# Attention with two expert layers: 64-query sets merged into one matmul pair, wider streams in the values' and first gate's matmuls, two groups of sums emitted later

## The chip, the core and the metric

The kernel runs on one core of one Trainium2 chip. The metric is device time in microseconds (us) of one execution, and lower is better. The engines are TensorE (PE for its matmuls, PEld for its weight loads), VectorE (DVE), ScalarE (ACT), GpSimd (POOL) and SyncE (SP, which only issues transfers here). TensorE's clock has two levels, 1.2 and 2.4 GHz; the profile gives the granted clock of a stretch as 0.50 or 1.00.

## What is computed

Windowed attention over 2 batches, 8 heads, 576 positions and 64 columns per head; then a first expert layer, which sends each of the 1152 tokens to the one expert that its gate prefers; then a second expert layer, in which every token goes through all 8 experts, weighted by a matrix that eight rounds of row and column scaling (the Sinkhorn steps) produce from the second gate.

```python
scores = where((rel >= 0) & (rel < 128), scale * q @ k.T + slope_h * (-abs(rel)), -1e9)
attn   = exp(scores - max) / (sum(exp) + 1e-9)
x      = (attn @ v)                                   # 1152 tokens x 512
...
e      = argmax(x @ w_gate, axis=1)                   # first gate; a token keeps its place below the capacity
x1[i]  = gate_w[i] * (relu(x[i] @ w1[e]) @ w2[e])     # first expert layer
...
P      = exp(x1 @ u_gate - max)                       # second gate
for _ in range(8):                                    # the Sinkhorn steps
    P /= P.sum(1, keepdims=True) + 1e-9
    P /= P.sum(0, keepdims=True) + 1e-9
    P *= N / E
out    = sum over e of P[:, e] * (relu(x1 @ u1[e]) @ u2[e])
```

## The kernel before

**Attention.** Queries go in blocks of at most 128. A batch has 576 positions, so it has four blocks of 128 and a last one of 64: of the ten blocks `t`, numbers 4 and 9 have 64 queries. A unit `u` is one block with four of the eight heads (two units per block, so units 8, 9, 18 and 19 are the 64-query sets). For each unit the steps are `scores` (PE), `pick`, `limit` (DVE), `powers` (ACT), `turn_p` (PE transposes of the probabilities), `take_p` (they are moved to SBUF as `pT`, by ACT, DVE and POOL), `values` (PE) and `norm` (DVE). The probabilities of one query block against the block before and against its own are two parts, and `values` adds both in PSUM: for a 64-query block the first part has 128 rows and the second has 64.

In `values` the stationary operand is `pT` of one head (128 or 64 columns wide), and the moving operand is 104 columns of the values (`WIDE`), of which 65 are used: 64 of the head and a column of ones that gives the sum of the powers. The last head of a block has only 65 columns left to stream. `norm` divides by that sum. An fp32 matmul shows in the trace as two records of the same shape.

**First gate.** `turn_x`, `take_x` and `logits` give the gate's logits of a block. The 8 columns of the gate's weights are streamed six times side by side (48 columns), of which the first 8 are read. `top`, `gate`, `choice`, `count`, `place`, `mark`, `table`, `add_table` find each token's expert and its place there (DVE, ACT and PE by turns). The first expert's tokens need no trip through memory for the last three blocks: `first_turn` and `first_add` (PE) put them together, and `first_split` (ACT, DVE) makes the high and low parts with which the first expert's matmuls begin.

**What sets the order there.** The steps up to this point stand in a list written out by hand, `ORDER`; each engine runs its instructions in that order.

**First experts**, lines 735 to 1024, then **the second layer's first expert** in three column chunks `j` (`hps` and `ops`, lines 1265 to 1328), with the second gate (`gate_2`: `lps`, `lsb`, `ltp`, `lga`), the Sinkhorn steps (`sinkhorn_start`, `sinkhorn_rows`, `sinkhorn_columns`; the matmul `cps` sums over partitions) taken one at a time from a list by `sink_next`, and two groups of sums for the other seven experts, which are computed with fewer products: `token_sums` (the tile `tsums`, DVE and ACT; the loop takes a few of its pieces at a time with `run(tsteps, ...)`) and `weight_sums` (the tile `sums`, POOL). Here no order is written out: a scheduler in the compiler places each engine's instructions by when it expects them to be ready, so that the place of a call in the code is not the place in the program.

**The other seven experts**, lines 1360 to 1395, are dense matmuls to the end.

Of the kernel before, what the change touches and what calls it, by code (L numbers as in the profile page):

```python
# [9 lines left out]
F32 = mybir.dt.float32  # L10
# [5 lines left out]
ALU = mybir.AluOpType  # L16
# [5 lines left out]
P = 128  # L22
FAST = 192
EPS = 1e-9
# [65 lines left out]
def fused_kernel(ctx, tc, q, k, v, wg1, w1, w2, wg2, u1, u2, out, capacity):  # L90
    nc = tc.nc
# [10 lines left out]
    blocks = [(b, s, min(P, S - s)) for b in range(B) for s in range(0, S, P)]  # L102
    NT = len(blocks)
    LATE = 3
    WIDE = 104
    NE = 3


# [139 lines left out]
    with ExitStack() as st:  # L248
# [174 lines left out]
        def head(g, i, j):  # L423
            return HG * g + 2 * j + i
# [65 lines left out]
        def take_p(a):  # L490

            u, i2 = a
            t, g = units[u]
            n = blocks[t][2]
            ptp = ppt[u][:, 2 * i2:2 * i2 + 2]
            pT = la.tile([P, 2, 2, P], F32, tag="pT", name="pT", bufs=4)
            if len(kparts[t]) == 1:
                nc.scalar.copy(pT[:, 0, :, :n], ptp[:, :, :n])
            else:
                for i, (tk, nk) in enumerate(kparts[t]):  # L500
                    out, mask = pT[:nk, i, :, :n], side[:nk, i:i + 1, :n].to_broadcast([nk, 2, n])
                    if i2 + i > 0:
                        nc.vector.tensor_tensor(out=out, in0=ptp[:nk, :, :n], in1=mask, op=ALU.mult)
                    else:
                        nc.scalar.copy(out, ptp[:nk, :, :n])
                        nc.gpsimd.tensor_tensor(out=out, in0=out, in1=mask, op=ALU.mult)
            pTd[u, i2] = pT

        def values(a):
            u, i2 = a  # L510
            t, g = units[u]
            n = blocks[t][2]
            if u not in xpd:
                xpd[u] = ps_x.tile([P, 2, 2 * P], F32, tag="xps", name="xps")
            for j in range(2):
                h = head(g, i2, j)
                at = h * (D + 1)

                cols = min(WIDE, (H - h) * (D + 1))
                for i, (tk, nk) in enumerate(kparts[t]):  # L520
                    nc.tensor.matmul(xpd[u][:n, i2, j * (D + 1):j * (D + 1) + cols], pTd[u, i2][:nk, i, j, :n],
                                     vb[tk].rearrange("p h d -> p (h d)")[:nk, at:at + cols],
                                     start=(i == 0), stop=(i == len(kparts[t]) - 1))

        def norm(u):
            t, g = units[u]
            n = blocks[t][2]
            xps = xpd[u]
            if t not in xd:
                xd[t] = wl.tile([P, H, D], F32, tag="x", name="x", bufs=LATE)  # L530
            xps = xps[:n, :, 0:2 * (D + 1)].rearrange("p i (j d) -> p i j d", j=2)
            rec = sm.tile([P, 2, 2, 1], F32, tag="rec", name="rec")
            nc.vector.tensor_scalar_add(rec[:n], xps[:, :, :, D:D + 1], EPS)
            yield
            nc.vector.reciprocal(rec[:n], rec[:n])
            yield
            nc.vector.tensor_tensor(out=xd[t][:n, HG * g:HG * (g + 1), :].rearrange("p (j i) d -> p i j d", i=2),
                                    in0=xps[:, :, :, 0:D], in1=rec[:n].to_broadcast([n, 2, 2, D]), op=ALU.mult)
# [15 lines left out]
        def logits(t):  # L554
            n = blocks[t][2]
            lgp = ps_t.tile([P, ND * P], F32, tag="pt", name="lgp")
            for c in range(ND):

                nc.tensor.matmul(lgp[:n, 0:6 * E], gt['xT', t][:, c, :n], wg1_sb[:, c:c + 1, :].to_broadcast([P, 6, E]),
                                 start=(c == 0), stop=(c == ND - 1))  # L560
            gt['lg', t] = lgp

# [694 lines left out]
    def run(steps, count=99):  # L1257
        for _ in range(count):
            if next(steps, 0) == 0:
                break  # L1260
# [4 lines left out]
    for j in range(NCH):  # L1265
        cols = slice(j * CH, (j + 1) * CH)
        hs = []
        hpss = {}

        def layer1(f, cs):  # L1270
            if f not in hpss:
                hpss[f] = ps_h.tile([P, CH], F32, tag="ph", name="hps2")
            f0 = (f % (NF // 2)) * P
            for c in cs:
                whi, wlo = wpair(i0 + f // (NF // 2), c, slice(f0, f0 + P))
                for m, (a, bb) in enumerate(((whi, y_hi), (whi, y_lo), (wlo, y_hi))):
                    nc.tensor.matmul(hpss[f], a, bb[c][:, cols], start=(c == 0 and m == 0), stop=(c == ND - 1 and m == 2))  # L1277

        if j == 0:

            for f in range(3):
                layer1(f, range(2))
        for f in range(NF):
            layer1(f, range(2, ND) if f in hpss else range(ND))
            hps = hpss[f]
            h_hi, h_lo = hidden(f)
            a_op = nc.scalar.activation(h_hi, hps, AF.Relu)
            v_op = nc.vector.scalar_tensor_tensor(out=h_lo, in0=hps, scalar=0.0, in1=h_hi.bitcast(F32),
                                           op0=ALU.max, op1=ALU.subtract)
            hs.append((h_hi, h_lo))  # L1290
            if j == 0:
                if f == 0:
                    gates[:] = [a_op.ins, v_op.ins]
                if f % 2 == 1:
                    split_next()
                if f == NF - 1:
                    gates.clear()
                    load_1(0)
            if f > 1 or j:
                sink_next()  # L1300
            if j and f % 2:
                run(tsteps, 1)
        if j == 0:
            weight_sums(0)
        if j == NCH - 1:
            run(tsteps)
            xsteps = parts_x(0)
        for i in range(TPC):
            s = j * TPC + i
            ops = ps_o.tile([P, DM], F32, tag="po", name="ops")  # L1310
            m = 0
            for f in range(NF):
                whi, wlo = wpair(i0 + 2 + f // (NF // 2), f % (NF // 2), slice(0, DM))
                h_hi, h_lo = hs[f]
                tcol = slice(i * P, (i + 1) * P)
                for a, bb in ((h_hi, whi), (h_hi, wlo), (h_lo, whi)):
                    nc.tensor.matmul(ops, a[:, tcol], bb, start=(m == 0), stop=(m == 3 * NF - 1))  # L1317
                    m += 1
                if f % 2:
                    sink_next()  # L1320
            if sink:
                late.append((s, ops))
            else:
                nc.vector.tensor_scalar_mul(acc[s], ops, Pm[:, s, 0:1])
            if j == NCH - 1:
                run(xsteps, 2)
                if i == 1:
                    run(token_sums_over())
            else:
                run(tsteps, 3)  # L1330
    assert not sink and not late

# [124 lines left out]
```

## Time and profile before

| | |
|---|---|
| median of three runs | 1049.8 us (1042.55 to 1054.35) |
| the profiled execution | 1049.41 us, of which 1047.2 us are its span |
| PE busy | 1028.1 us of the span |
| DVE, ACT, POOL busy | 673.8, 387.0, 319.4 us |
| mean granted clock of TensorE | 0.989 |

The rows further down come from the profiled execution, and their times count from its span's start. A row of the timeline gives start, duration, engine, line, operation, out<-in, rows*columns of the stationary operand, the output's shape and the number of records that were merged into it; in square brackets stands the idle time of the engine before it and what ended it. Attention and gate fill the first 115.7 us, the first experts run to about 274 us, the second layer follows.

### The profile page before, as it was taken

The page shows a single profiled execution, that of the slowest core. Times are in us where ns is not written, and L with a number is a line of the kernel's source. Part 1 is how long each engine was busy: PE and PEld are TensorE (multiplying, and loading weights), DVE is VectorE, ACT ScalarE, POOL GpSimd, SP SyncE. Part 2 cuts the span into 40 slices and gives each one's busy share as a digit, 9 for nine tenths or more (in the row PEclk, how much of TensorE's full clock was granted, in tenths as well). Part 3 has the DMA queues.
Part 4 walks back from the last instruction along what each step waited for, and adds up shares of the span by engine and source line. Part 5 has one row for each costly group of instructions (what it writes and reads, how often), then busy time and mean ns, then how long its engine had stood idle before and what let it go on. Part 6 is the DMA issues. An engine that isn't in the chain of part 4 may idle for free.

```text
span 1047.2 us, 16893 instructions
## 1 busy us (share of the span) xinstructions
PE 1028.1 (98%) x6420; PEld 936.7 (89%) x6420; DVE 673.8 (64%) x1636; ACT 387.0 (37%) x838; POOL 319.4 (30%) x305
## 2 busy tenths in 40 slices
PE   8999999999999999999999999999999999999997
PEld 6888999999889988999998989999998989999896
DVE  7987677877795336575757566575756556575752
ACT  6643367777431214232323323232323313232320
POOL 6533144441200032422413133232413233232213
PEclk9998799999999999999999999999999999999999
DMA  9921379797300021120202111120201111020102
GB/s 226 225 61 57 111 213 268 204 251 243 121 1 1 1 81 42 41 81 1 82 4 78 41 41 43 39 81 1 82 21 61 41 41 64 18 81 1 41 1 90
DMA packets 74104, 83.24 MB, mean 79 GB/s; under 512 B 31585, under 2 KB 45921, under 8 KB 74018
## 3 DMA queue, kind: packets, MB, share of 16 engines
q1 hardware_dynamic: 71906, 76.59, 24.9%
q0 software_dynamic: 2112, 5.52, 1.8%
q8 instruction: 52, 0.85, 0.3%
q14 instruction: 34, 0.28, 0.1%
HBM read 77.37 MB, written 4.73 MB: 78 GB/s over the span
## 4 chain that ended last, share of the span: by engine, by line
PE 71%; issue 2%; DVE 1%; POOL 1%; POOLq 0%; ACT 0%; ACTq 0%
PE pr L1391 31%; PE pr L1360 29%; PE ops L1317 5%; PE hps L1277 4%; PE pb L748 1%; POOL out_dram L1395 1%; PE pb L752 1%; DVE wlo L191 0%; DVE tsums L1163 0%; POOL w_wlo L1254 0%; PE lps L1050 0%; POOLq L1453 0%; PE cps L1087 0%; DVE lsb L1054 0%; PE ltp L1057 0%
## 5 line engine op out<-in xcount | busy, mean ns | idle before, releaser
L1391 PE MATMUL pr<-w_whi,hT 128*128 128x512 f32 x1008 | 315.8, 390 | 0.3 <-DVE hT L1352 0.3
L1391 PEld LDWEIGHTS pr<-w_whi,hT 128*128 128x128 f32 x1008 | 189.2, 188 | 39.6 <-DVE hT L1352 0.5
L1391 PE MATMUL pr<-w_wlo,hT 128*128 128x512 f32 x504 | 196.4, 390 | 0.0
L1254 POOL TENSOR_TENSOR w_wlo<-r,w_whi 128x512 fp32r<-128x512 f32 x56 | 71.4, 1294 | 291.9 <-ACT w_whi L1253 182.0
L1393 DVE SCALAR_TENSOR_TENSOR acc<-pr,Pm,acc 128x512 f32<-128x512 f32 x126 | 91.3, 744 | 91.0 <-PE pr L1391 90.9
L1351 ACT ACTIVATE hT<-pr 128x256 fp32r<-128x256 f32 (+1 forms) x168 | 69.0, 411 | 174.4 <-DVE pr L1368 174.4
L1352 DVE SCALAR_TENSOR_TENSOR hT<-pr,hT 128x256 fp32r<-128x256 f32 (+1 forms) x168 | 77.0, 458 | 80.1 <-ACT hT L1351 80.1
L1360 PE MATMUL pr<-y_hi,wy 128*128 128x320 f32 (+1 forms) x560 | 122.6, 297 | 0.0
L1391 PEld LDWEIGHTS pr<-w_wlo,hT 128*128 128x128 f32 x504 | 94.6, 188 | 19.5 <-POOL w_wlo L1254 0.4
L1360 PEld LDWEIGHTS pr<-y_hi,wy 128*128 128x128 f32 x560 | 93.8, 188 | 0.3 <-DVE hT L1352 0.3
L1247 POOL TENSOR_TENSOR wy<-r,wy 128x512 fp32r<-128x512 f32 x28 | 39.9, 1426 | 174.3 <-ACT wy L1246 174.3
L191 DVE TENSOR_TENSOR wlo<-w,whi 128x1024 fp32r<-128x1024 f32 x66 | 82.0, 1245 | 3.1 <-issue 3.1
L1360 PE MATMUL pr<-y_lo,wy 128*128 128x256 f32 (+1 forms) x280 | 83.2, 297 | 0.0
L748 PE MATMUL pb<-xt,whi 128*128 128x384 f32 x256 | 74.2, 361 | 2.5 <-issue 2.0
L179 ACT CAST whi<-w 128x1024 fp32r<-128x1024 f32 x66 | 69.1, 1050 | 19.9 <-DMA w<-in_moe_w_dram 15.4
L748 PE MATMUL pb<-h,whi 128*128 128x384 f32 x256 | 75.3, 361 | 0.6 <-DVE t L768 0.6
L1253 ACT CAST w_whi<-r 128x512 fp32r<-128x512 f32 x56 | 33.1, 619 | 96.0 <-PE pr L1391 95.1
L1351 ACT ACTIVATE hT<-h 128x256 fp32r<-128x256 f32 (+1 forms) x56 | 24.9, 445 | 115.4 <-DVE h L1368 115.4
L1360 PE MATMUL pr<-y_hi,wx_wlo 128*128 128x256 f32 (+1 forms) x224 | 64.6, 288 | 0.0
L1360 PE MATMUL pr<-y_hi,wx_whi 128*128 128x256 f32 (+1 forms) x224 | 64.4, 288 | 0.0
L1360 PE MATMUL pr<-y_lo,wx_whi 128*128 128x256 f32 (+1 forms) x224 | 64.4, 287 | 0.0
L1231 POOL TENSOR_TENSOR sums<-r 128x512 f32<-128x512 f32 x28 | 37.1, 1326 | 77.7 <-DMA r<-in_moe_w_dram 49.4
(358 smaller groups left out, 2269.7 us busy)
## 6 DMA issues: line engine op xcount, KB each, us to landing
w<-in_moe_w_dram SPq DMA_DIRECT2D x36, 1024.0 KB, 7.0
r<-in_moe_w_dram SPq DMA_DIRECT2D x56, 512.0 KB, 3.8
kb<-in_k_dram SPq DMA_DIRECT2D x8, 256.0 KB, 4.1
qb<-in_q_dram SPq DMA_DIRECT2D x8, 256.0 KB, 4.7
vb<-in_v_dram SPq DMA_DIRECT2D x8, 256.0 KB, 6.8
xg_d<-xg SPq DMA_DIRECT2D x8, 256.0 KB, 2.2
kb<-in_k_dram SPq DMA_DIRECT2D x2, 128.0 KB, 4.1
qb<-in_q_dram SPq DMA_DIRECT2D x2, 128.0 KB, 3.5
```

Of the source, the lines that this page charges most:

```text
L179: nc.scalar.copy(his[i][:, sl, :], raws[i][:, sl, :])
L191: nc.vector.tensor_tensor(out=los[i][:, sl, :], in0=raws[i][:, sl, :], in1=his[i][:, sl, :].bitcast(F32), op=ALU.subtract)
L748: nc.tensor.matmul(ps[:, 0:2 * W], whi, x.rearrange("p r w -> p (r w)"), start=(m == 0), stop=(m == K - 1))
L1247: nc.gpsimd.tensor_tensor(out=wy[1][:, i], in0=x, in1=wy[0][:, i].bitcast(F32), op=ALU.subtract)
L1254: nc.gpsimd.tensor_tensor(out=w2p[1][:, k], in0=x, in1=w2p[0][:, k].bitcast(F32), op=ALU.subtract)
L1277: nc.tensor.matmul(hpss[f], a, bb[c][:, cols], start=(c == 0 and m == 0), stop=(c == ND - 1 and m == 2))
L1317: nc.tensor.matmul(ops, a[:, tcol], bb, start=(m == 0), stop=(m == 3 * NF - 1))
L1351: nc.scalar.activation(hi, src, AF.Relu)
L1352: nc.vector.scalar_tensor_tensor(out=lo, in0=src, scalar=0.0, in1=hi.bitcast(F32), op0=ALU.max, op1=ALU.subtract)
L1360: nc.tensor.matmul(ps, a[:, i, c, f], b, start=(c == 0 and m == 0), stop=(c == 1 and m == 2))
L1391: nc.tensor.matmul(ops, a[:, k, s * P:(s + 1) * P], b[:, k, :], start=(m == 0), stop=(m == 6 * QP - 1))
L1393: nc.vector.scalar_tensor_tensor(out=acc[s], in0=ops, scalar=Pm[:, s, e:e + 1], in1=acc[s], op0=ALU.mult, op1=ALU.add)
```

## The change

Four edits.

1. `WIDE` is 128: the values' matmuls stream 128 columns (104 so far); of these 65 are used as before.
2. `logits` streams the gate's weights 15 times, 120 columns (6 times, 48 columns, so far).
3. For a 64-query block, `take_p` lays the two heads' `pT` side by side, 2 x 64 columns, and `values` multiplies both at once with the values of both heads (130 columns): one matmul with a stationary operand 128 wide where there were two with 64. Each head's result stands in its own 64 partitions, so `norm` takes the sums and the products in two instructions each, one for every head half; the reciprocal stays one.
4. `weight_sums(0)` is called after the last column chunk's first layer (so far after the first chunk's), and `token_sums` gets no steps in the first chunk.

```diff
-    WIDE = 104
+    WIDE = 128
...
             pT = la.tile([P, 2, 2, P], F32, tag="pT", name="pT", bufs=4)
+            if 2 * n <= P:
+                pT = pT[:, :, 0, 0:2 * n].rearrange("p i (j q) -> p i j q", j=2)
...
+            if 2 * n <= P:
+                h = head(g, i2, 0)
+                for i, (tk, nk) in enumerate(kparts[t]):
+                    nc.tensor.matmul(xpd[u][:2 * n, i2, 0:2 * (D + 1)].rearrange("p (j d) -> p j d", j=2),
+                                     pTd[u, i2][:nk, i].rearrange("p j q -> p (j q)"),
+                                     vb[tk][:nk, h:h + 3:2, :], start=(i == 0), stop=(i == len(kparts[t]) - 1))
+                return
...
+            if 2 * n <= P:
+                rec = sm.tile([P, 2, 1], F32, tag="rec", name="rec")
+                both = [slice(j * n, (j + 1) * n) for j in range(2)]
+                for j, rows_ in enumerate(both):
+                    nc.vector.tensor_scalar_add(rec[rows_], xps[rows_, :, j * (D + 1) + D:(j + 1) * (D + 1)], EPS)
+                yield
+                nc.vector.reciprocal(rec[:2 * n], rec[:2 * n])
+                yield
+                to = xd[t][:n, HG * g:HG * (g + 1), :].rearrange("p (j i) d -> p i j d", i=2)
+                for j, rows_ in enumerate(both):
+                    nc.vector.tensor_tensor(out=to[:, :, j, :], in0=xps[rows_, :, j * (D + 1):j * (D + 1) + D],
+                                            in1=rec[rows_].to_broadcast([n, 2, D]), op=ALU.mult)
+                return
...
-                nc.tensor.matmul(lgp[:n, 0:6 * E], gt['xT', t][:, c, :n], wg1_sb[:, c:c + 1, :].to_broadcast([P, 6, E]),
+                nc.tensor.matmul(lgp[:n, 0:15 * E], gt['xT', t][:, c, :n], wg1_sb[:, c:c + 1, :].to_broadcast([P, 15, E]),
...
-        if j == 0:
-            weight_sums(0)
         if j == NCH - 1:
             run(tsteps)
+            weight_sums(0)
             xsteps = parts_x(0)
...
-            else:
+            elif j:
                 run(tsteps, 3)
```

What the built program makes of it stands at three places. On PE, the first of the second batch's two 64-query sets (`vb` are the values of the two key blocks, `ptp` the transposed probabilities, `lgp` the gate's logits, `xtp` the transposed block). Before:

```order
L545 MATMUL xtp<-ident,x 128x128 x4
L521 MATMUL xps<-vb_985,pT 64x104
L521 MATMUL xps<-vb_1471,pT 64x104
L521 MATMUL xps<-vb_985,pT 64x104
L521 MATMUL xps<-vb_1471,pT 64x104
L521 MATMUL xps<-vb_985,pT 64x104
L521 MATMUL xps<-vb_1471,pT 64x104
L521 MATMUL xps<-vb_985,pT 64x104
L521 MATMUL xps<-vb_1471,pT 64x104
L488 MATMUL ptp<-ident,pr 128x64 x2
L559 MATMUL lgp<-wg_sb,xT 128x48 x4
```

And now:

```order
L569 MATMUL xtp<-ident,x 128x128 x4
L522 MATMUL xps<-vb_985,pT 128x130
L522 MATMUL xps<-vb_1467,pT 128x130
L522 MATMUL xps<-vb_985,pT 128x130
L522 MATMUL xps<-vb_1467,pT 128x130
L488 MATMUL ptp<-ident,pr 128x64 x2
L583 MATMUL lgp<-wg_sb,xT 128x120 x4
```

Eight matmuls of a set have become four, which still go to and fro between the two key blocks; nothing has moved past them. The same holds for the other three sets.

On POOL, in the second layer, the first expert's weight sums (`r` are raw weights) and the maximum over partitions (`gma`) with which the Sinkhorn steps begin. Before:

```order
L922 UNCONDITIONAL_BRANCH
L1231 TENSOR_TENSOR sums<-r_5729 128x512 x2
L1231 TENSOR_TENSOR sums<-sums,r_5729 128x512
L1231 TENSOR_TENSOR sums<-r_5729,sums 128x512
L1067 ISA
L1067 ISA gma<-gm 128x1
```

And now:

```order
L946 UNCONDITIONAL_BRANCH
L1255 TENSOR_TENSOR sums<-r_5721 128x512 x2
L1255 TENSOR_TENSOR sums<-sums,r_5721 128x512
L1255 TENSOR_TENSOR sums<-r_5721,sums 128x512
L1091 ISA
L1091 ISA gma<-gm 128x1
```

Nothing has moved here: the sums still stand ahead of the maximum.

On DVE, from the gate's maximum per partition (`gm`) on, with the token sums (`tsums` and the tiles they go to, `t`, `y_lo`), the second layer's hidden values (`h`) and the first Sinkhorn step (`ngm`, `rs`). Before:

```order
L1065 TENSOR_REDUCE gm<-lg_5513 128x1
L1160 TENSOR_TENSOR t_1_5524<-tsums,t_0_5523 128x256
L1069 TENSOR_SCALAR ngm_5668<-gma 128x1
L1160 TENSOR_TENSOR y_lo_1985<-tsums,y_hi_1981 128x256
L1163 TENSOR_TENSOR tsums<-y_hi_1981,y_lo_1985 128x256
L1076 TENSOR_REDUCE rs<-Pm 128x9
L1188 TENSOR_TENSOR tsums<-tsums 128x256
```

And now:

```order
L1089 TENSOR_REDUCE gm<-lg_5505 128x1
L1184 TENSOR_TENSOR t_1_5516<-tsums,t_0_5515 128x256
L1184 TENSOR_TENSOR y_lo_1977<-tsums,y_hi_1973 128x256
L1187 TENSOR_TENSOR tsums<-y_hi_1973,y_lo_1977 128x256
L1200 TENSOR_TENSOR tsums<-tsums 128x256
L1312 SCALAR_TENSOR_TENSOR h__5653<-hps_5640,h__5653 128x384
L1212 TENSOR_TENSOR tsums<-tsums 128x256
L1184 TENSOR_TENSOR y_lo_1976<-tsums,y_hi_1972 128x256
L1187 TENSOR_TENSOR tsums<-y_hi_1974,y_lo_1978 128x256
L1184 TENSOR_TENSOR t_1_5516<-tsums,t_0_5515 128x256
L1204 TENSOR_TENSOR tsums<-tsums 128x256
L1093 TENSOR_SCALAR ngm_5660<-gma 128x1
```

The token sums have not moved later: ahead of `gm` DVE's rows are the same as before, and behind it nine more rows of token sums and hidden values stand ahead of `ngm`. From `gm` to the first column sum of the Sinkhorn steps (`cs`) DVE has 22 rows now (14 so far), and on PE the first `cps` stands eight matmuls of `ops` later than it did; from there to the second `cps` there are 18 matmuls, as before.

## Rows read from the trace of the kernel before

**Rows 1.** The page: busy time of PE, and the granted clock in 40 slices.

```profile
PE 1028.1 (98%) x6420; PEld 936.7 (89%) x6420; DVE 673.8 (64%) x1636; ACT 387.0 (37%) x838; POOL 319.4 (30%) x305
PEclk9998799999999999999999999999999999999999
```

**Rows 2.** Stretches (start:end, length, each engine's busy time, clock, DMA share, GB/s).

```profile
52.00:59.00 7.00, 7.00 (x56) 4.84 (x55) 3.10 (x22) 2.89 (x8) 1.37 (x2) 1.00 0.47 90
59.00:91.90 32.90, 32.05 (x334) 28.91 (x333) 31.49 (x183) 16.83 (x54) 12.84 (x16) 1.00 0.20 57
91.90:98.73 6.83, 6.74 (x48) 4.88 (x48) 4.18 (x25) 2.38 (x8) 2.31 (x3) 1.00 0.18 59
98.73:112.39 13.66, 13.66 (x66) 11.58 (x66) 6.12 (x42) 1.08 (x5) 1.04 (x1) 0.50 0.05 20
...
115.80:119.21 3.41, 3.41 (x14) 3.41 (x14) 0.89 (x4) 1.16 (x2) 1.32 (x2) 0.50 0.49 128
...
289.88:293.29 3.41, 3.41 (x13) 2.76 (x12) 1.98 (x7) 0.41 (x1) 0.00 (x0) 0.50 0.00 0
```

**Rows 3.** Timeline of PE: values (L521), logits (L559), the first expert's tokens (L675, L683).

```profile
52.30 2.64 PE L521 MATMUL xps<-vb,pT 128*64 128x104 f32 x16
...
62.23 0.67 PE L559 MATMUL lgp<-wg_sb,xT 128*64 128x48 f32 x8
...
81.91 1.04 PE L521 MATMUL xps<-vb,pT 128*128 128x104 f32 x8
...
92.05 1.09 PE L559 MATMUL lgp<-wg_sb,xT 128*128 128x48 f32 x8
...
97.93 3.55 PE L521 MATMUL xps<-vb,pT 128*64 128x104 f32 x16
101.41 2.02 PE L675 MATMUL pt<-ident,xw 128*128 128x96 f32 x8
...
105.96 1.09 PE L559 MATMUL lgp<-wg_sb,xT 128*64 128x48 f32 x8
...
107.62 2.91 PE L683 MATMUL pt<-slots,x 128*128 128x192 f32 x8
...
115.72 0.64 PE L748 MATMUL pb<-xt,whi 128*128 128x384 f32 x1 [0.25 <-DVE xt L237]
```

**Rows 4.** Groups by form in 94.05 to 96.64 us, one 64-query set (busy, mean ns).

```profile
L521 PE MATMUL xps<-vb,pT 128*64 128x104 f32 x8 | 1.6, 278 | 0.1
L521 PE MATMUL xps<-vb,pT 64*64 64x104 f32 x8 | 1.6, 275 | 0.0
```

**Rows 5.** Groups by form: tokens' matmuls in 112.99 to 114.3 us.

```profile
L683 PE MATMUL pt<-slots,x 64*128 64x192 f32 x8 | 1.6, 336 | 0.0
```

**Rows 6.** Groups by form in 10 to 116 us: the values that stream 104 columns.

```profile
L521 PE MATMUL xps<-vb,pT 128*128 128x104 f32 x196 | 27.7, 278 | 1.6 <-DVE pT L503 0.7 <-DVE x L537 0.7 <-DVE pos L625 0.2
```

**Rows 7.** Timeline of DVE: `norm` behind a 64-query set, and a 64-row product.

```profile
54.98 0.15 DVE L533 TENSOR_SCALAR rec<-xps 64x4 f32<-64x4 f32 x1 [2.10 <-PE xps L521]
...
55.45 0.41 DVE L537 TENSOR_TENSOR x<-xps,rec 64x256 f32<-64x256 f32 x1
...
90.82 0.28 DVE L503 TENSOR_TENSOR pT<-ptp,side 64x128 f32<-64x128 f32 x1
```

**Rows 8.** Timeline of POOL and DVE where the second layer begins.

```profile
280.58 3.51 POOL L1231 TENSOR_TENSOR sums<-r 128x512 f32<-128x512 f32 x2 [24.45 <-DVE wlo L191]
...
285.21 2.80 DVE L1163 TENSOR_TENSOR tsums<-y_hi,y_lo 128x256 f32<-128x256 f32 x2
...
303.72 0.28 DVE L1081 TENSOR_REDUCE cs<-Pm 128x8 f32<-128x72 f32 x1
```

**Rows 9.** The chain that ended last, 293 to 340 us (start, length).

```profile
300.10 4.21 PE ops L1317 x18
304.30 0.21 PE cps L1087 x2
```

## The prediction

> **What bounds the kernel now.** I read the page first: PE is busy in 1028.1 of 1047.2 us, and the strip of granted clocks is full but for two dents [rows 1]. So time is won or lost where PE works at the lower clock or waits, and the change touches only the first 116 us and the stretch around 280 to 320. Next the stretches: PE worked 13.66 us at 0.50 from 98.73 on and was busy all of that time, 3.41 us more from 115.80, and 3.41 us from 289.88 [rows 2]. That is 20.5 of 1047.2 us at half speed; everything else ran at 1.00, the first batch's 64-query sets at 52 to 59 us too [rows 2]. Ahead of the long fall (91.90 to 98.73) PE was busy 6.74 of 6.83 us, with a 64-query set, a round of logits and the start of the next set. Third, the timeline of PE: from the last 64-query set (97.93) to the first matmul of the first experts (115.72) 17.8 us pass [rows 3]. From there on PE is dense, so that what is won ahead of 115.72 should arrive at the end. Nothing in the change touches the other seven experts.
>
> **Merged sets.** A set of 16 records took 2.64 us at the full clock [rows 3], and is to have 8. Eight records with a weight twice as wide take 1.04 us where all have 128 rows [rows 3]: the lower bound. The upper bound is no gain, 2.64. The 64-query sets alternate between operands of 128 and of 64 rows [rows 4], in eight pairs of records, 2.64 / 8 = 0.33 us each, which is slower per record (0.165) than the wider records of the dense sets (1.04 / 8 = 0.13); so something is paid at every turn. The merged set still alternates [the order in the section on the change], in four pairs, each with a quarter more columns. 4 x 0.33 x 1.25 = 1.65 us is my value, 1.0 us less for each set, of a possible 0 to 1.6. On DVE `norm` has one small instruction more (0.15) and two products where there was one (0.41): the nearest row for 64 x 128 elements takes 0.28 [rows 7], so 0.15 + 2 x 0.28 - 0.41 = 0.30 us more for each set. It lies on the path: DVE waits for the set (2.10 us at 54.98 [rows 7]) and is busy 31.49 of the 32.90 us that follow block 4 [rows 2]; the result goes on to the next transposes. All four sets: 4 x (-1.0 + 0.3) = -2.8 us.
>
> **128 columns instead of 104.** 196 records are widened [rows 6]. If columns set their time, a record would grow by 24/104 of 0.13 us, 0.03 us, 5.9 us in all. But eight records of logits with 48 columns take 1.09 us and eight of values with 104 take 1.04 [rows 3]: twice the columns for no more time, so the 128-wide weights that both load set it. With 192 columns eight records take 1.6 us [rows 5], 0.2 each; in proportion 128 columns would be 0.133 us, hardly above 0.13. I take 0.003 x 196 = +0.5 us, from 0 to 5.9. A rule speaks against that: the Trainium skill ("TensorE: Matmul & The Clock Gate", Part 3, "What overlaps and what doesn't") says that a weight load overlaps a running matmul only if the two use different row groups, and these records use the same rows one after the other. By it the columns would come on top of the load, and this term would be at its upper end. The equal times of 48 and 104 columns disagree with it.
>
> **120 columns of logits.** Eight of ten rounds have 128-wide weights, which cover 120 columns as they cover 104: 0. The two rounds of 64 queries load 64-wide weights, and eight records took 0.67 us at the full clock [rows 3]; 120 columns would take 120/192 of 1.6, 1.0 us: +0.33 each, +0.7 (0 to 0.8).
>
> **The stretch at half clock.** What changes ahead of the fall at 98.73 is what PE does there: half as many records in the sets, each twice as wide, and logits of 120 columns. The same mixture of sets and logits stood at 52 to 59 us at the full clock [rows 2], so it is not always followed by a fall, and no row says whether the new mixture is. I choose that the clock stays up until the first experts begin; the first rival is that it doesn't. Prices at both levels: the 64-query logits 1.09 against 0.67, eight token records 2.91 against 1.6 [rows 3, 5], that is 0.55 to 0.61 of the time. With 0.6 the 13.66 us lose 5.5. Not all could go: behind the last set stands a chain through DVE and ACT (norm, transposes, logits, top, choice, count, place, token matmuls) which doesn't run by PE's clock and becomes what is late next; 0.6 rather than 0.5 leaves it 1.4 us.
>
> **The two short falls.** 115.80 and 289.88 cost 3.41 x 0.5 = 1.7 us each. Ahead of both PE waits (for the first expert's parts; for DVE's copy `lsb`), and the change leaves both waits where they are. The fall need not come each time: the three runs of the same program lie 11.8 us apart. I count one of two gone, -1.7 us, from -3.4 to +1.7.
>
> **Later sums.** The diff moves them, the program doesn't: POOL's order is the same, and the token sums still begin behind the first copy of the logits [the orders in the section on the change]. So the slow part stays: while POOL makes the weight sums (3.51 us for two from 280.58), DVE needs 2.80 us for two token sums [rows 8]. Only the Sinkhorn steps move. `cs` stands eight DVE rows later, about 0.35 us each, 2.8 us; its reader `cps` stands eight matmuls later, 8 x 4.21/18 = 1.9 us [rows 9]. Between later steps DVE has the same 4.2 us as before: `cs` ended at 304.00 and `cps` ran at 304.30 [rows 8, 9]. PE may wait once, 0 to 1.2 us; with the 0.3 us that were spare I take 0.5.
>
> **Sum.** Against the profiled execution's own 1049.4 us (0.4 under the median): -2.8 + 0.5 + 0.7 - 5.5 - 1.7 + 0.5 = -8.3, which gives 1041.1; I forecast **1041**.
>
> **Rivals.**
> - *The clock falls all the same* near 98 us, since DVE's chain leaves PE with small work there. Then only the sets, widths and logits count: -2.8 + 0.5 + 0.7 + 0.5 = -1.1, and the short falls as they were: 1048. For it: PE was fully busy before the fall, so being busy alone didn't hold the clock. Against it: the stretch at 52 to 59 us, which held it with narrower records.
> - *Every fall goes*, and the merged sets reach 1.04 us: -8.3 - 1.7 - 4 x 0.6 = -12.4, 1037. For it: the fastest of the three runs, 1042.55, shows that some 7 us go by falls that needn't come.
> - *Slower*: the clock falls at the first batch's sets, at 52 to 59 us, where it held before, because there PE now has half as many records and then waits for DVE, which has more to do. If it stays low as long as it did (13.66 us), that is 5.5 us more, on top of the case in which the second fall stays: 1048 + 5.5, about 1053.5. It decides if the half clock begins before 90 us. Against it: the sets are followed at once by dense scores and values.
> - *The columns count* (the rule above): each of 196 records 0.025 to 0.03 us longer, +5.4 against my term: 1046.5. For it there is only that no row shows 128 columns between such loads.
> - *The change does less than it says* is for the later sums my forecast already. If the scheduler's new order did spare PE's wait near 286 us, some 2 to 3 us more would go: 1038.5.
>
> **How the numbers follow.** Forecast 0.45, clock falls all the same 0.20, every fall gone 0.18, slower 0.06, columns count 0.05, sums help 0.06. One per cent, 10.5 us, is about what a measurement of this kernel can tell from no change: faster means under 1039.3, slower over 1060.3. Under 1039.3 lie the third and the last case and a third of the forecast's own spread of some 3 us: 0.18 + 0.05 + 0.15 = 0.38. Over 1060.3 lies only a fall much longer than the one seen, 0.03. The rest is 0.59. The range runs from 1034 (every fall gone, and a little more) to 1049 (the long fall stays, with the wait at `cps`).
>
> **What would show it.** Right: eight records per 64-query set in 1.5 to 1.8 us; eight wide values still near 1.04 and eight logits near 1.1 us; a clock of 1.00 through 90 to 106; the first experts' matmuls at 106 to 109 us; POOL's sums ahead of `gma`, and no new wait at `cps`. Wrong: half clock from before 100 us (first rival), a fall before 90 us (third), eight values at 1.2 us or more (fourth), or a gain that shows at 108 us and is given back in the first experts, where the weights' transfers would have to come sooner by as much.

## The result, and the profile after

The changed kernel takes 1039.26 us (median of 10 runs, 1035.78 to 1043.16) against 1048.64 us (10 runs, 1042.55 to 1054.35): a ratio of 0.9902, 95% interval 0.9880 to 0.9924. The forecast was 1041, with a range from 1034 to 1049. The profiled execution took 1038.18 us, of which 1036.1 are its span. Runs more than 1.5% over the fastest of their kernel are left out throughout; these are five of the 29 runs of the kernel before in the second group below, with mean clocks of 0.981 to 0.987, and with them the slope given below would be 0.91 instead of 0.865.

From the page of the changed kernel, busy times and the granted clock in 40 slices, against [rows 1]:

```profile
PE 1018.7 (98%) x6388; PEld 930.3 (90%) x6388; DVE 677.8 (65%) x1644; ACT 387.3 (37%) x838; POOL 315.5 (30%) x305
PEclk9999999999999999999999999999999999999999
```

The dents are gone. PE has 32 records fewer, two for each of the sixteen matmuls that the merge took out. Stretches of the changed kernel, against [rows 2] (same columns):

```profile
52.00:59.00 7.00, 6.90 (x59) 5.39 (x55) 5.18 (x34) 3.26 (x9) 1.38 (x2) 1.00 0.60 118
59.00:91.94 32.94, 31.72 (x320) 28.62 (x320) 31.15 (x177) 16.59 (x53) 12.86 (x16) 1.00 0.19 55
91.94:98.76 6.82, 6.60 (x42) 5.09 (x40) 4.60 (x29) 2.59 (x10) 2.53 (x4) 1.00 0.18 59
98.76:108.61 9.85, 9.60 (x80) 8.40 (x79) 8.29 (x46) 2.33 (x6) 0.67 (x1) 1.00 0.20 69
109.39:112.80 3.41, 3.41 (x15) 3.21 (x14) 0.43 (x3) 0.62 (x2) 1.86 (x2) 0.50 0.71 214
```

What stood at 0.50 for 13.66 us now runs at 1.00. One short fall is left, at the start of the first experts; the one of the second layer (289.88 before) did not come in this execution. (Both kernels also end at 0.50, from 1044.23 us before and from 1034.4 now.) The timeline of PE, against [rows 3]:

```profile
52.71 1.65 PE L522 MATMUL xps<-vb,pT 128*128 128x130 f32 x8
...
61.52 1.04 PE L583 MATMUL lgp<-wg_sb,xT 128*64 128x120 f32 x8
...
88.99 1.06 PE L532 MATMUL xps<-vb,pT 128*128 128x128 f32 x8
...
91.94 1.15 PE L583 MATMUL lgp<-wg_sb,xT 128*128 128x120 f32 x8
...
97.11 1.72 PE L522 MATMUL xps<-vb,pT 128*128 128x130 f32 x8 [0.19 <-DVE x L552]
98.76 1.13 PE L699 MATMUL pt<-ident,xw 128*128 128x96 f32 x8
...
101.41 1.04 PE L583 MATMUL lgp<-wg_sb,xT 128*64 128x120 f32 x8
...
108.61 0.45 PE L772 MATMUL pb<-xt,whi 128*128 128x384 f32 x1 [0.25 <-DVE xt L237]
```

A merged set takes 1.65 to 1.75 us, eight wide values 1.06, eight logits 1.15 (128-wide weights) and 1.04 (64-wide): the four durations that the prediction named. The first experts start at 108.61 (115.72 before), inside its 106 to 109. `norm` on DVE, against [rows 7]:

```profile
54.40 0.33 DVE L546 TENSOR_SCALAR rec<-xps 64x2 f32<-64x2 f32 x2 [1.02 <-PE xps L522]
...
55.18 0.59 DVE L552 TENSOR_TENSOR x<-xps,rec 64x128 f32<-64x128 f32 x2
```

That is 0.92 us for what was 0.15 + 0.41, 0.36 more; the prediction had 0.30.

The first experts' start comes 7.1 us sooner, the end of the span 11.1. Of the other 4.0 us, 1.4 is the fall that stayed away (3.41 us at the lower clock). Another 2.0 is a place of which the prediction knew nothing. The timeline of PE in the kernel before, in the first experts, eight records behind a jump of PE's program to its last part (the first row; `PEq` is PE's sequencer):

```profile
254.22 0.59 PE L748 MATMUL pb<-xt,whi 128*128 128x384 f32 x2 [0.30 <-PEq L922]
...
257.54 0.52 PE L748 MATMUL pb<-xt,whi 128*128 128x384 f32 x2 [1.96 <-issue]
```

PE stands for 1.96 us, and no semaphore, engine or transfer is named for it. At the same matmul the changed kernel's row has no wait:

```profile
247.63 0.54 PE L772 MATMUL pb<-xt,whi 128*128 128x384 f32 x2
```

In the second layer PE's waits for `lsb` fell from 2.27 us in two waits to 2.08 in one. POOL's first sums and DVE's token sums still meet, against [rows 8] (timelines of POOL, DVE and PE, one row each):

```profile
274.43 3.23 POOL L1255 TENSOR_TENSOR sums<-r 128x512 f32<-128x512 f32 x2 [26.07 <-DVE wlo L191]
...
277.87 2.92 DVE L1187 TENSOR_TENSOR tsums<-y_hi,y_lo 128x256 f32<-128x256 f32 x2
...
281.30 0.35 PE L1081 MATMUL ltp<-ident,lsb 16*128 16x16 f32 x3 [2.08 <-DVE lsb L1078]
```

### The profile page after: what moved, and what is told of

Same layout as the page of the kernel before. It is cut to its first block, busy times and chain, and to the rows that moved or that the text cites. A ratio compares the mean times of both kernels' runs of the same rounds, so it can differ in the third digit from the quotient of the medians.

```text
span 1036.1 us, 16836 instructions
## 1 busy us (share of the span) xinstructions
PE 1018.7 (98%) x6388; PEld 930.3 (90%) x6388; DVE 677.8 (65%) x1644; ACT 387.3 (37%) x838; POOL 315.5 (30%) x305
## 4 chain that ended last, share of the span: by engine, by line
PE 72%; issue 2%; POOL 1%; DVE 1%; POOLq 0%; ACT 0%
PE pr L1414 31%; PE pr L1383 30%; PE ops L1340 5%; PE hps L1301 5%; PE pb L772 1%; POOL out_dram L1418 1%; PE pb L776 1%; PE lps L1074 0%; DVE tsums L1187 0%; POOL w_wlo L1278 0%; PE cps L1111 0%; POOLq L1476 0%; DVE lsb L1078 0%; DVE y_lo L1184 0%; PE ltp L1081 0%
```

## The experiments

Twelve kernels, in three groups of four; each group has its own runs of the kernel before on the same chip. Since the clock changes from run to run, two numbers are read for each kernel beside its median: the mean granted clock over its runs, and the time that it would take at full clock. For the second, one straight line was laid through 193 runs of all kernels, with a value of its own for each kernel and one common slope: **0.865 us (standard error 0.04) for each thousandth that the mean clock falls short of 1**. A thousandth of 1040 us is 2.1 us at half clock, so that a microsecond there costs 0.42 us; the prediction had worked with 0.4 for the long fall and 0.5 for the short ones. The values at full clock have a standard error of 0.5 to 0.7. A difference between groups is also one between chips: the kernel before itself comes out at 1040.3 to 1042.3.

| kernel | median, us | ratio to before, 95% | mean clock | at full clock | its group's before |
|---|---|---|---|---|---|
| sets undone | 1047.5 | 0.9965 (0.994 to 0.999) | 0.9962 | 1044.4 | 0.9897, 1042.3 |
| widths undone | 1045.5 | 0.9946 (0.9913 to 0.9978) | 0.9895 | 1036.8 | same |
| sums undone | 1040.0 | 0.9873 (0.9841 to 0.9905) | 0.9968 | 1037.0 | same |
| gate copy on ACT | 1041.3 | 0.9886 (0.9855 to 0.9916) | 0.9957 | 1037.5 | same |
| changed, again | 1039.2 | 0.9908 (0.9877 to 0.994) | 0.9970 | 1036.4 | 0.9916, 1040.3 |
| records put back | 1041.1 | 0.9926 (0.9901 to 0.9951) | 0.9975 | 1039.4 | same |
| first batch merged | 1042.4 | 0.9959 (0.993 to 0.9988) | 0.9967 | 1039.8 | same |
| sums behind maximum | 1039.2 | 0.9926 (0.9898 to 0.9953) | 0.9960 | 1036.5 | same |
| logits narrow | 1043.7 | 0.9926 (0.9893 to 0.9958) | 0.9922 | 1036.3 | 0.9893, 1040.8 |
| values narrow | 1038.3 | 0.9891 (0.9841 to 0.994) | 0.9972 | 1036.5 | same |
| second batch merged | 1041.4 | 0.9929 (0.99 to 0.9958) | 0.9967 | 1039.1 | same |
| sums behind Sinkhorn | 1034.6 | 0.9842 (0.9797 to 0.9887) | 0.9990 | 1033.5 | same |

**Changed, again.** Run once more in the second group, so that others stand beside it on one chip.

> The changed kernel itself, so that the others of this group have it beside them. Expected: 1039 to 1040, mean granted clock 0.995 to 0.998.

**Sets undone.** Edit 3 taken back, in `take_p`, `values` and `norm`.

```diff
-            if 2 * n <= P:
+            if 2 * n <= 0:
```

> The changed kernel with edit 3 undone (64-query sets of 16 records again), wide streams and later sums kept. Theory W (the wide streams hold the clock): granted clock 1.00 from 88 to the first experts, which begin near 110.5 us (108.6 plus 4 x 0.5 at most for the sets, of which only the second batch's two arrive); time 1040 to 1041. Theory S (the merged sets hold it): half clock for about 14 us from near 98 us, first experts at 115 to 116, time about 1046. Theory B (both are needed): as S here.

The clock stayed at 1.00 from 88 us to the first experts, which began at 110.83: theory W, as far as the clock goes. The time did not follow it: 1047.5, where 1041 was expected, and the excess is at full clock. The theory let two sets arrive; all four do (**Which sets**, below). Another part is the stand at the jump, which is here as it was before (timeline of PE):

```profile
253.63 0.51 PE L772 MATMUL pb<-xt,whi 128*128 128x384 f32 x2 [1.99 <-issue]
```

**Widths undone.** Edits 1 and 2 taken back.

```diff
-    WIDE = 128
+    WIDE = 104
-                nc.tensor.matmul(lgp[:n, 0:15 * E], gt['xT', t][:, c, :n], wg1_sb[:, c:c + 1, :].to_broadcast([P, 15, E]),
+                nc.tensor.matmul(lgp[:n, 0:6 * E], gt['xT', t][:, c, :n], wg1_sb[:, c:c + 1, :].to_broadcast([P, 6, E]),
```

> The changed kernel with edits 1 and 2 undone (104 and 48 columns), merged sets and later sums kept. Theory W: half clock from between 92 and 99 us for 10 us or more, first experts at 113 to 115, time 1044 to 1046. Theory S: clock 1.00 up to the first experts, which begin at 107 to 108.5 us, time 1037 to 1039. Theory B: as W here.

A fall of 13.65 us came, so the merged sets alone don't hold the clock (S is out), but at 55.88 us, not between 92 and 99; why it comes there, and at 98.73 in the kernel before, is open. Mean clock as low as before; at full clock as good as the changed kernel. So the two halves of the change do different things: the merge saves time at either clock, the widths keep the clock.

**Which width.** Only the logits' 48 columns, and only the values' 104, put back.

> The changed kernel with the first gate's logits at 48 columns again (edit 2 undone), values at 128. With both widths undone the mean clock was 0.990, with both kept 0.997. Theory V (the 196 values records hold the clock): mean clock 0.995 or more, time within 1 us of the changed kernel's 1039. Theory L (the 80 logits records do): mean clock 0.990 to 0.992, time 1044 to 1046. If both count: between, 1041 to 1043.

> The changed kernel with the values at 104 columns again (edit 1 undone), logits at 120. Theory V: mean clock 0.990 to 0.992, time 1044 to 1046. Theory L: mean clock 0.995 or more, time 1038.5 to 1039.5.

Theory L. With narrow logits the mean clock is 0.9922 and the fall stands at 55.88 again; with narrow values it is 0.9972 and the time the changed kernel's. Stretches of the kernel with narrow logits (columns as above), and in the last row of the changed kernel, where no fall follows:

```profile
49.05:55.88 6.83, 6.83 (x62) 5.66 (x60) 5.52 (x28) 3.97 (x12) 2.24 (x4) 1.00 0.59 118
55.88:69.54 13.66, 13.66 (x75) 11.62 (x76) 8.02 (x47) 4.54 (x16) 1.96 (x4) 0.50 0.24 59
91.90:111.60 19.70, 19.12 (x151) 16.20 (x148) 16.00 (x95) 6.63 (x20) 4.40 (x5) 1.00 0.21 68
...
49.05:55.88 6.83, 6.83 (x63) 5.81 (x62) 5.55 (x27) 3.33 (x11) 2.24 (x4) 1.00 0.69 153
```

and of the one with narrow values, from the last record of scores to the first experts:

```profile
88.01:108.06 20.05, 19.58 (x152) 16.45 (x148) 15.99 (x95) 6.64 (x20) 4.60 (x5) 1.00 0.19 62
```

With merged sets the 80 logits records, 1.15 us for eight, decide; with those wide, the 196 values records make no difference. With narrow logits the mean clock is 0.9922 with wide values and 0.9895 with narrow ones, a difference that the scatter of the runs (an error of 0.002) doesn't tell from nothing. No run has wide logits with the unmerged sets and narrow values of the kernel before. At full clock the three variants of width and the changed kernel lie within 0.5 us of each other.

**Which sets.** Merged only for the first batch (the diff), and only for the second (`t > 4`).

```diff
-            if 2 * n <= P:
+            if 2 * n <= P and t < 5:
```

> The changed kernel with only the first batch's 64-query sets merged (blocks of the second batch as before). Theory: the first batch's gain of some 1.8 us is gone before 90 us, since DVE sets the pace there; the first experts begin within 0.5 us of where they do with no merged set (110.8), and the time stays 1.5 to 2.5 us above the changed kernel, apart from the 2 us stand of PE, which may or may not be there. Rival: the prediction's sum, by which each of the four sets gives 0.7 us: first experts at 109.5 to 110.

> The changed kernel with only the second batch's 64-query sets merged. Theory: these two sets give nearly all of the merge's gain up to the first experts, which begin at 108.5 to 109 us after scores that end at 88 to 89 as before; time 1039 to 1040, apart from PE's stand of up to 2 us at the jump in its instruction stream (16 records more than the changed kernel). Rival: first and second batch give alike; first experts at 109.5 or later, 1041.

By their starts the first experts, at 110.37 and 107.95 us, seem to bear the theory out: nothing from the first batch, all from the second. But these times count from the span's start, and the profiles differ before any 64-query set has run. Up to the third round of logits PE's program is the same in nine of these kernels, and that round begins anywhere from 42.82 us (second batch merged) to 45.96 (changed, again). So the stretches are taken between points of PE's own program, in us:

| kernel | third round of logits to last scores (holds the first batch's sets) | last scores to first experts (holds the second batch's) |
|---|---|---|
| before | 43.32 | 27.56, of which 13.66 at half clock |
| sets undone | 44.55 | 22.51 |
| first batch merged | 42.70 | 22.50 |
| second batch merged | 44.56 | 20.57 |
| changed | 42.68 | 20.56 |

The rows for sets undone and for the changed kernel (timelines of PE; the first experts' row of the latter stands above):

```profile
43.77 1.15 PE L583 MATMUL lgp<-wg_sb,xT 128*128 128x120 f32 x8
88.32 0.75 PE L444 MATMUL sps<-kS,qT 64*64 64x192 f32 x12
110.83 0.44 PE L772 MATMUL pb<-xt,whi 128*128 128x384 f32 x1 [0.25 <-DVE xt L237]
...
45.37 1.15 PE L583 MATMUL lgp<-wg_sb,xT 128*128 128x120 f32 x8
88.05 0.74 PE L444 MATMUL sps<-kS,qT 64*64 64x192 f32 x12
```

So the first batch's pair gives 1.87 us and the second's 1.95, all at full clock: the rival, by which the two give alike, is right, and the theory is wrong. In the first stretch the eight profiles with both widths and the first batch merged lie between 42.68 and 42.71; in the second those with the second batch merged lie between 20.28 and 20.62. Unmerged, these sets stream 128 columns as well and take longer than in the kernel before (first batch, timelines of PE in sets undone and in the kernel before; its first set took 2.64 [rows 3]):

```profile
51.21 2.96 PE L532 MATMUL xps<-vb,pT 128*64 128x128 f32 x16
55.70 2.75 PE L532 MATMUL xps<-vb,pT 128*64 128x128 f32 x16
...
56.41 2.51 PE L521 MATMUL xps<-vb,pT 128*64 128x104 f32 x16
```

That is 0.56 us for a pair, so that against sets of 104 columns a merged pair gives some 1.35. PE itself saves 2.34 us in a pair (2.96 and 2.75 against 1.65 and 1.72) and gives part of it back, in the first batch by a wait of 0.53 us for its own scores. The whole times, 1042.4 and 1041.4, are 3.4 and 2.7 us over the changed kernel at full clock, of which the sets explain 1.9 each; the profiles have PE wait 2.3 and 2.4 us for DVE's `t` in the first experts, against 0.4 and 0.7 in the changed kernel.

**Records put back.** Sixteen small matmuls ahead of the first transposes.

```diff
+            for _ in range(0 if kpt else 16):
+                nc.tensor.matmul(pt[:16, 0, :8], ident[:, :16], ident[:, :8], start=True, stop=True)
```

> The changed kernel with 16 small extra fp32 matmuls (16 columns of weights, 8 streamed) at the very start, while PE waits for the first keys, so that PE's instructions are again as many as before the merge. Theory F: the 1.96 us in which PE stood in the first experts (257.54 us before, nothing released it) depends only on where in PE's instruction stream the jump to the last two experts falls; then a stand of about 2 us comes back near record 1890, and the time is 2 us above the changed kernel. Rival: it belonged to the 64-query sets' timing or was chance; then no such stand and the changed kernel's time within 1 us.

The stand is back, at record 1891 (1890 in the kernel before and with the sets undone), 1.73 us:

```profile
247.37 0.44 PE L774 MATMUL pb<-xt,whi 128*128 128x384 f32 x1 [1.73 <-DVE t L794]
```

The profile puts it down to DVE's `t` this time, because that semaphore came last; the place is the same, and in the changed kernel nothing waits there. Over all fourteen profiles the rule holds: the three kernels with 6420 PE records have the stand, eight or nine records behind the jump, and none of the eleven with 6388 or 6404 has it. At full clock 3.0 us over the changed kernel, with 1.7 in this row. Theory F.

**Sums undone.** Edit 4 taken back (the diff of the change in reverse).

> The changed kernel with edit 4 undone (weight sums called after the first chunk's first layer, three token-sum steps in the first chunk). Theory: the edit moved nothing that PE waits for, so the time is that of the changed kernel, within 1 us of 1039, and PE waits about 2 us in all for the copies of the second gate's logits, as both kernels do. Rival: the edit removed the short half-clock stretch of the second layer; then it is back here, 280 to 292 us, and the time is 1041 or more.

1040.0, at full clock 0.6 over the changed kernel, which ran on another chip. Against the kernel before on its own chip it gains 5.3 us and the changed kernel 3.9: the same within the error of some 1.2. PE waits 2.3 us for `lsb`. A short fall at 280.42 us was there; but it was at 282.45 in the second profile of the changed kernel too, so edit 4 doesn't decide it.

**Gate copy on ACT.**

```diff
-            nc.vector.tensor_copy(lsb, lps[:2 * E, :])
+            nc.scalar.copy(lsb, lps[:2 * E, :])
```

> The changed kernel with the copy of the second gate's logits (lsb) made by ScalarE instead of VectorE, nothing else. Theory: PE's wait of 2.08 us at 281.3 is the copy standing in VectorE's queue behind token sums that take 2.9 us for two because GpSimd's weight sums run at the same time; ScalarE is idle there for 4.6 us, so the wait goes and the time is 1037 to 1038. Rival: PE then waits as long one step later (the copies lga on VectorE, the maximum over partitions, the first column sum): 1039, no difference.

No gain: 1041.3, at full clock 1037.5. The wait stayed where it was, now for ACT (timelines of ACT and of PE):

```profile
283.31 0.40 ACT L1183 CAST y_hi<-tsums 128x256 fp32r<-128x256 f32 x1 [3.94 <-DVE tsums L1200]
283.62 0.46 ACT L1078 COPY lsb<-lps 16x384 f32<-16x384 f32 x1
...
284.14 0.35 PE L1081 MATMUL ltp<-ident,lsb 16*128 16x16 f32 x3 [2.15 <-ACT lsb L1078]
```

ACT was idle, as the theory said, but its queue was not free: ahead of the copy stood a cast that waited 3.94 us for the same slow token sums.

**Sums behind the maximum.** What edit 4's words say, made to happen.

```diff
-        nc.gpsimd.partition_all_reduce(gma, gm, P, bass.bass_isa.ReduceOp.max)
+        raw1['gma'] = nc.gpsimd.partition_all_reduce(gma, gm, P, bass.bass_isa.ReduceOp.max)
...
-            weight_sums(0)
+            with tc.issue_after(raw1['gma'].ins): weight_sums(0)
```

> The changed kernel with GpSimd's weight sums tied behind the maximum over partitions with which the Sinkhorn steps begin, so that they really run later. Theory: token sums on VectorE then take 0.35 to 0.4 us each around 275 to 280, the copy lsb is made in time, PE's wait of 2.08 us before the last ltp falls under 0.5 us; time 1.5 to 2 us under the changed kernel. Rival: PE then waits elsewhere (at cps, with GpSimd's sums beside the Sinkhorn steps), no difference.

Both the theory's gain and the rival's wait came. The wait for `lsb` is gone and PE has the second layer's first part (261.88 to 284.17) dense in 22.29 us; then the sums meet the Sinkhorn steps (timelines of POOL, DVE and PE):

```profile
286.80 2.81 POOL L1255 TENSOR_TENSOR sums<-r 128x512 f32<-128x512 f32 x2 [7.04 <-ACT y_hi L1183]
...
287.09 1.39 DVE L1212 TENSOR_TENSOR tsums<-tsums 128x256 f32<-128x256 f32 x1
288.41 1.29 DVE L1103 TENSOR_TENSOR Pm<-Pm,rs 128x72 f32<-128x72 f32 x1
...
291.10 0.27 DVE L1105 TENSOR_REDUCE cs<-Pm 128x8 f32<-128x72 f32 x1
...
291.52 0.57 PE L1111 MATMUL cps<-cs,ones_f 128*128 128x8 f32 x2 [3.00 <-DVE cs L1105]
```

DVE's product of `Pm` takes 1.29 us instead of 0.23, and PE waits 3.00 us at `cps`; 6.83 us at the lower clock follow, from 290.95. The gain was given back there.

**Sums behind Sinkhorn.** So the sums were tied behind the last Sinkhorn step, where the scaled matrix is done (`late.clear()`).

```diff
-                late.clear()
+                late.clear(); raw1['gma'] = nc.gpsimd.tensor_copy(sk.tile([P, 1], F32, tag="gm", name="done"), Pm[:, 0, 0:1])
...
-            weight_sums(0)
+            with tc.issue_after(raw1['gma'].ins): weight_sums(0)
```

> The changed kernel with GpSimd's weight sums tied behind the last Sinkhorn step (through a one-column copy on GpSimd), later than in the run in which they stood behind the maximum. Theory: what cost PE 2.1 us at ltp and there 3.0 us at cps was VectorE slowed by GpSimd's sums (0.41 us products took 1.39); now neither wait is left, second layer's first matmul to the first matmul of the other experts takes 106.5 to 107.5 us (109.2 in the changed kernel), time 1036 to 1037.5. Rival: the sums then come late for the next expert's parts, and PE waits for those: 1039 or more.

1034.6 us, below what the theory said, 4.6 under the changed kernel's median and the fastest of all (at full clock 3.0 under the one with narrow values, on the same chip); all six runs between 1032.7 and 1035.5, each with a mean clock of 0.999. The stretches, second layer's first matmul to its first `ops`, and on to the other experts:

```profile
263.94:286.23 22.29, 22.29 (x133) 19.70 (x132) 17.33 (x48) 8.27 (x18) 0.43 (x1) 1.00 0.04 12
286.23:370.49 84.26, 84.26 (x425) 75.25 (x424) 39.92 (x121) 16.65 (x35) 14.10 (x12) 1.00 0.08 26
```

Together 106.55 us, PE busy in all of it (109.15 in the changed kernel). Two token sums take 0.75 us again:

```profile
277.11 0.75 DVE L1187 TENSOR_TENSOR tsums<-y_hi,y_lo 128x256 f32<-128x256 f32 x2
```

and POOL's sums begin at 329.17, with no one waiting for them. Besides the 2.1 us of the wait, this kernel kept the clock in every run, where the changed kernel's runs had 0.993 to 0.999.

## Why the prediction was right, point by point

- **The sum.** Forecast -8.3, measured -9.4. Split by the group with both kernels on one chip: the clock 4.7 us (0.9916 to 0.9970), the time at full clock 3.9 (1040.3 to 1036.4). In the other groups the kernel before ran at 0.989, and the clock's part would be 6.3 to 6.7. The prediction had -7.2 for clock and -1.1 for the rest. So the clock was put 0.5 to 2.5 us too high and the rest 2.8 too low (the split has a standard error of 0.8), and the total is near in part by luck: what the rest lacked is above all the stand, below.
- **Merged sets, -2.8.** Right, in mechanism and size. The records' time and `norm` came as priced (1.65 to 1.75 us; +0.36), and all four sets arrive: 1.87 and 1.95 us for the two pairs. That is against unmerged sets of 128 columns; against those of 104, which are 0.28 us shorter each, 2.7 are left.
- **What was not in the sum: -2.0,** PE's stand at the jump, which the merge removed by taking 32 records out of PE's program ahead of it. That the stand follows the number of records is shown by putting them back. The step that the prediction lacked is here: it took PE as dense from the first experts on, so that a microsecond won ahead of them is one at the end. These 2.0 came without having been forecast.
- **128 columns, +0.5.** Right: eight records 1.06 against 1.04 us, and from the third round of logits to the last scores, a stretch with 98 of the 196 records, 42.68 us with 128 columns and 42.56 with 104, about 0.25 in all. The rival that the columns count is out. The rule that stood for it is the Trainium skill's ("TensorE: Matmul & The Clock Gate", Part 3, "What overlaps and what doesn't"): a weight load overlaps a running matmul only on other row groups. The trace disagrees with it as it did before.
- **120 columns of logits, +0.7.** 0.37 for each 64-query round, 0.33 forecast; the eight other rounds, put at nothing, take 0.06 more each (1.15 against 1.09).
- **The stretch at half clock, -5.5.** Right in size: with the sets undone and the clock held, the stretch from the last scores takes 22.51 us instead of 27.56, 5.05 less, and that kernel's wider sets and logits cost up to 1.1 there by their rows. The reason was left open between set and logits; with the sets merged, the runs give it to the logits' 120 columns alone.
- **The first rival** (the clock falls all the same, near 98 us) did not come, not even without the widths. **The slower rival**'s place was real: with merged sets and 48-column logits the fall does come at the first batch's sets, at 55.88 us, for 13.66 us; but then it comes there in place of 98 us, not on top of it, so that it makes nothing slower than before.
- **The short falls, -1.7.** One of two, in this execution; that it would be one was a guess. Of the fourteen profiles eight have a short fall in the second layer, each at or behind a wait of PE of 1.7 us or more (for `lsb` or `cps`); five with such a wait have none. In the kernel without either wait none of six runs lost more than a thousandth. The fall at the start of the first experts, in six profiles, stands ahead of that wait, and no run tells what brings it.
- **Later sums, +0.5.** Right that the edit moves nothing that matters (no difference beyond the error); the half microsecond at `cps` did not come. The last rival's price, 2 to 3 us if PE were spared the wait near 286, was right as well, but it needed sums that really move.

Open: at full clock, sets undone lies 7.4 us (standard error 0.9) over sums undone on the same chip; the stand (2.0) and the four sets (3.8) explain 5.8. The rest is not explained: both profiles have waits for `t` of about the same size (2.5 and 3.0 us). That it lies 2.1 us over the kernel before, which has unmerged sets too, fits the widths' price at full clock by the rows: 1.1 for the four sets, 1.2 for the logits and 0.25 for the other values.

## What to carry to other kernels

A change of a per cent in a kernel whose clock moves is two changes: read the mean clock of every run, and ask of each edit what it does at full clock and what it does to the clock. An edit at a call's place in the code moves nothing until the built order shows it; when work on GpSimd is moved for VectorE's sake, move it past everything that waits for VectorE, not just past the first such wait. And measure a stage between two points of one engine's program, not from the start of the span: with the same program up to there, PE reached the third round of logits up to 3.1 us apart, more than the 1.9 that a pair of merged sets is worth, and by the times from the start one pair seemed to give nothing.

## What the runs showed of the hardware

- PE can stand for 1.7 to 2.0 us behind a jump in its own program, and whether it does hangs on how many instructions stand ahead. The Trainium skill ("Advanced Engine Details and Errata", "Control Flow Timing") gives about 51 ns for an unconditional branch; here it was 0.30 us at the jump and 1.96 eight records later.
- A DVE instruction with two operands in SBUF took 1.29 to 1.56 us beside GpSimd's sums instead of 0.23 to 0.48: 0.9 to 1.1 us more, and about as long as one of GpSimd's own instructions (1.26 to 1.40 us). The sum `cs` with one operand kept its 0.27. The Trainium skill ("SBUF — State Buffer", "SBUF: two separate sides") says that the two engines share a pair of ports, which one instruction holds whole; the rows agree.
- Eight logits records with 120 instead of 48 columns take 0.06 us more, 1.15 against 1.09; the 80 of this kernel are worth 4 us of clock (mean clock 0.997 against 0.992). PE was fully busy in either case: 6.83 of 6.83 us from 49.05 to 55.88, after which the clock fell with 48 columns and stayed with 120.
